# Third block of four: another order of the w1 quads, sums read in place, and a fifth group of w2 in seven products

## The chip, the core and the metric

One core of a Trainium2 chip runs the whole kernel. The metric is the device time of one execution in microseconds; the median of three runs is given. A kernel's profile comes from one further execution.

## What is computed

Cut to what matters (x has 2048 rows of 1024; 1024 states; w1 is 1024 x 3584, w2 is 3584 x 1024):

```python
xn = layernorm(x)
Lam_bar = exp(dt * Lam)                       # complex, one per state
Bu = xn @ (((Lam_bar - 1) / Lam)[:, None] * Bmat).T
h[t] = Lam_bar * h[t - 1] + Bu[t]             # recurrence over the 2048 rows
A = 2 * Re(h @ Cmat.T) + xn * Dskip
m = xn @ w1 + b1
B = (m * tanh(softplus(m))) @ w2              # mish, then the second layer
out = x + A + B
```

## The kernel before, in words

The 2048 rows are worked in four blocks of 512. In each block TensorE makes three kinds of product: the first layer (w1), the projections into and out of the recurrence (B and C), and the second layer (w2, called dense). Every product of 128 x 128 weights goes through PSUM, which has eight banks of 512 columns. VectorE does the recurrence: it rotates the projections (`rotate_in`, L914), scans them (`scan`, L1451), rotates back (`recur`, L1458). ScalarE applies mish, scales and evacuates banks.

The four blocks differ. The first multiplies plainly. In the second, four of seven quads of w1 are done with seven half-size products in place of eight; in the third and fourth all seven quads are, and the projections as well. A quad is a set of 512 rows of the hidden layer. Each of its seven products (n = 1 to 7) needs one unit of weights of 256 KB: n = 1, 2, 4 are raw pieces of w1, and n = 5, 7, 6, 3 are sums and differences of pieces, which VectorE makes once (`w_sums`, L1191). All units lie in DRAM (`wsd`), and each block fetches them again through a ring of seven slots of 512 KB, filled by SP (`ring_load`, L426; `ring_fill`, L856). A slot is refilled when PE has used it. An item of the ring is a pair of units, in the order of use.

The sums of quads 0, 1 and 2 are made in the third block itself: a step `k0` makes the next one on VectorE and POOL stores it (those of quad 2 are stored by SP, step `O0`). Before, the third block took the quads in the order 3, 4, 5, 6, 0, 1, 2 (`REAL`, L207), and fetched every unit from `wsd`, those just made too.

The second layer of the third and fourth block is done partly in seven products too. There the 28 tiles of the hidden layer are split in halves 0 to 13 and 14 to 27; a group is two tiles of each half. `NFG` (L186) says how many groups a block does in seven products: 4 in the third, all 7 in the fourth. The remaining tiles of the third block are multiplied plainly, in pairs (`PLAIN`, L189), 8 matmuls of 512 columns per tile. For the seven products a group's four rows of w2 are loaded raw by POOL (`d2_load`, L1219), scaled by ScalarE (`d2_row`, L1233), summed by VectorE (more `k0` steps) and stored in `w2d`; the hidden tiles are scaled (`act_scale`, L896) and summed (`act_sums`, L1339; `CHUNKS`, L1323). Group 4, which the fourth block needs, was made while its tiles passed through the ring in the third block's plain part (`PASSING`, L190).

The order of the third block is a string, `STEPS` (L196), of steps such as p1 (product 1 of the first quad; p q s w x y z are the seven quads in order of work, a b c d the projections), k0, g (mish), G (scale two hidden tiles), h (scale a row of w2), m (load rows of w2), r (rotate), E (statistics of the next block's x), l0 (load that x, by POOL), t (sums of the hidden tiles). A product and its evacuation were one step. What follows the last product stood in the code: `dense_part` (L1589) and the loop over `recur`. Its PE order is the seven products 1, 7, 2, 5, 6, then the plain pairs, then 3 and 4, then the projection out, j = 0 to 7.

Each engine runs its own instructions in the order in which the steps issue them, and waits on semaphores only where a buffer is not yet written or still read. Banks count as buffers: product 6 of a quad waits until product 1 in the same bank has been read out.

Of the kernel before, what the change touches and what calls it, by code (L numbers as in the profile page):

```python
# [9 lines left out]
P = 128  # L10
# [153 lines left out]
def build_kernel(nc, A_x, A_Lambda_re, A_Lambda_im, A_B_re, A_B_im, A_C_re, A_C_im,  # L164
# [27 lines left out]
    WHOLE = ("a2 a1 V0 b2 b1 a5 b5 V1 P4 P5 a6 b6 v6 P6 P7 a3 b3 P0 a7 b7 P1 Q0 n0 p1 q1 a4 b4 "  # L192
# [6 lines left out]
    LAST = ("p1 p5 p2 q1 q5 p6 q2 s1 p7 s5 p3 q6 s2 M5 p4 q7 q3 k0 k0 s6 q4 g0 K0 a2 a1 k0 s7 k0 s3 O0 O0 O0 O0 m6 b2 b1 s4 G1 G0 g1 a5 G3 b5 G2 a6 b6 "  # L199
# [7 lines left out]
    REAL = (3, 4, 5, 6, 0, 1, 2)  # L207
    UNITS = [(REAL[QUADS.index(o[0])], int(o[1])) for o in STEPS.split() if o[0] in QUADS]
    W_ITEMS = [("ws", tuple(UNITS[i:i + 2])) for i in range(0, len(UNITS), 2)]
    ON_CHIP = [(5, n) for n in (5, 6, 3, 7)]  # L210
    OPENS = [(REAL[QUADS.index(o[0])], int(o[1])) for o in WHOLE.split() if o[0] in QUADS]
    OPENS = [u for u in OPENS if u not in ON_CHIP]
    O_ITEMS = [("w1", f // 2) for f in TILES[::2]] + [("ws", tuple(OPENS[i:i + 2])) for i in range(0, len(OPENS), 2)]

# [197 lines left out]
    items = []  # L412
    for blk in range(NB):
        items += W_ITEMS if blk in SPLIT else O_ITEMS if blk == FAST else [("w1", g) for g in range(NF // 2)]
# [8 lines left out]
        items += [("c", j) for j in range(NJ)] if blk >= FAST else []  # L423
    n_loaded = [0]
# [175 lines left out]
    def plain_root():  # L600
        aop(lambda e: e.activation(ln[:, 3, :], mv[:, :, 1], AF.Sqrt, bias=kon[:, 2:3]), reads=b_mv + [b_kon], writes=b_ln[3])
        vop(lambda e: e.reciprocal(ln[:, 3, :], ln[:, 3, :]), reads=b_ln[3], writes=b_ln[3])
# [247 lines left out]
    n_item = [0]  # L850

    def item_done():
        n_item[0] += 1
        ring_fill()
# [8 lines left out]

    def first_tile(blk, f):
        bank = f % 8
        raw = blk == 0 and f < NR
        if raw:
            first_rest(f)
        for k in range(0 if raw else NK):
            s, w = w1_tile(n_item[0], f % 4, k)  # L870
            PE.mm(lambda e, k=k, w=w: e.matmul(ps[:, bank, :], lhsT=w, rhs=xnT[:, k, :],  # L871
                                               start=k == 0, stop=k == NK - 1),
                  reads=[b_ring[s]] + b_xnT, writes=[b_ps[bank]], first=k == 0, last=k == NK - 1)
        if f % 4 == 3:
            item_done()
            item_done()
        at = place(blk, f)
        ts = slice(2 * P if raw else 0, 4 * P)
        aop(lambda e: e.activation(at[0][:, ts], ps[:, bank, ts], AF.Mish, bias=b1(f)),
            reads=[b_ps[bank], b_par], writes=[at[1]])  # L880
# [113 lines left out]
    def w_out(blk, i, ci):  # L994
        f0 = 4 * i + 2 * ci
        return f0, *(places(SPLIT[0], f0, 2) if blk in SPLIT else places(blk, 4 * REAL[i] + 2 * ci, 2))

    def w_product(blk, i, n):
# [3 lines left out]
        direct = blk == FAST and (REAL[i], n) in ON_CHIP  # L1002
        if direct:
            unit, b_unit = w_unit(w_raw(REAL[i], *((1, 1), (0, 0), (0, 1), (1, 0))[(5, 6, 3, 7).index(n)]))
        else:
            kind, units = items[n_item[0]]
            s, half = n_item[0] % NRING, units.index((REAL[i], n))
            assert n_item[0] < n_loaded[0]
# [18 lines left out]
        if not direct and half == len(units) - 1:  # L1027
            item_done()

    def w_evacuate(blk, i, n, keep):  # L1030
        X, Y, Z = (F_BANKS if blk == FAST else W_BANKS)[i]
        at = REAL[i]
# [156 lines left out]
    steps, later, held = [], [], []  # L1189
# [21 lines left out]
    D2_RAW += [(("a", 24), ("a", 10)), (("h", 0), ("h", 4)), (("h", 8), ("h", 12))]  # L1211
# [21 lines left out]
    def d2_row(n, slot=None):  # L1233
# [4 lines left out]
        if slot is not None:  # L1238
            x, b_x = ring[:, slot, j * D:(j + 1) * D].rearrange("p (d t) -> p d t", d=2), [b_ring[slot]]
        aop(lambda e: e.activation(o, x, AF.Copy, scale=wg[:, r:r + 1]),  # L1240
            reads=b_x + [b_wg], writes=b_t[2 * j:2 * j + 2])
# [5 lines left out]

    def d2_scale(g):
        for n in range(4):
            d2_row(4 * g + n)  # L1250
# [72 lines left out]
    CHUNKS = {2: ((0, 8),), 3: ((0, 6), (6, 12), (12, 14))}  # L1323
# [44 lines left out]
    def project_fast(blk, order, open_unit):  # L1368
        keep = {}
        for o in order.split():  # L1370
            kind, n = o[0], int(o[1:])
            if kind == "r":
                rotate_in(n)
            elif kind == "u":
                open_unit(n)
            elif kind == "G":
                act_scale(blk, n)
            elif kind == "g":
                mish(blk, n)
            elif kind == "k":  # L1380
                if steps or later:
                    some(1)
                    ring_fill()
            elif kind == "e":
                if later:
# [654 lines left out]
```

## Time and profile before

| | |
|---|---|
| three timed runs, us | 588.10, 587.55, 587.74 |
| median, us | 587.74 |
| profiled execution: span, us | 586.3 (no other time of it is shown) |
| busy: VectorE, ScalarE, POOL | 88%, 69%, 26% of the span |
| granted TensorE clock | 1.000 |
| moved by DMA | 162.15 MB, mean 277 GB/s |

The span runs from the first to the last instruction of the profiled execution, the timed runs include what lies around it. Third block: from about 306.9 to 446.9 us. A line of a timeline gives the start in us, the time from the first start to the last end, the engine, the source line, the operation, the tiles written and read, and how many instructions were merged; a bracket says how long the engine had been idle and whom it waited for. Of a matmul, records can be missing.

### The profile page before, as it was taken

Reading aid. Unit: us, or ns where it says so; the run is one execution under the profiler, and the core shown is the slowest. Engines: PE = TensorE matmul, PEld = TensorE weight load, DVE = VectorE, ACT = ScalarE, POOL = GpSimd, SP = SyncE. Lnnn points to the kernel's source line nnn. Section 1 sums busy time; section 2 is a strip of 40 time slices with the busy share of each in tenths; the row PEclk is TensorE's granted clock in tenths of the full one; section 3 lists DMA queues with packets and bytes.
Section 4 is the critical chain, followed back from the end, with each engine's and each line's share of the span. In section 5 each row is a group of like instructions: output and inputs, shape, how many; then the busy total and the mean of one; then the engine's idle time right before and its main releaser. Section 6 shows DMA issues by size and latency. Waiting matters only on the chain.

```text
span 586.3 us, 9768 instructions
## 1 busy us (share of the span) xinstructions
PE 581.0 (99%) x3599; PEld 353.9 (60%) x3635; DVE 513.4 (88%) x789; ACT 401.8 (69%) x541; POOL 150.7 (26%) x213
## 2 busy tenths in 40 slices
PE   9999999999999999999999999999999999999998
PEld 8644444444447887444448888644446888844444
DVE  6998999998997878999877889779999669789995
ACT  4859994658578868999916687959223798992330
POOL 2899300123524420441351241001010113100000
PEclk9999999999999999999999999999999999999999
DMA  9999998999688978999999899798865966998832
GB/s 244 306 243 247 245 186 202 316 301 360 185 303 287 357 249 293 316 321 255 345 375 345 305 309 382 257 344 209 306 210 191 346 237 241 326 324 318 293 113 73
DMA packets 116345, 162.15 MB, mean 277 GB/s; under 512 B 55882, under 2 KB 66762, under 8 KB 116298
## 3 DMA queue, kind: packets, MB, share of 16 engines
q1 hardware_dynamic: 99776, 109.67, 62.0%
q0 software_dynamic: 13440, 44.57, 21.7%
q10 hardware_dynamic: 3082, 7.29, 3.3%
q8 instruction: 29, 0.48, 0.3%
q14 instruction: 18, 0.15, 0.1%
HBM read 115.36 MB, written 34.08 MB: 255 GB/s over the span
## 4 chain that ended last, share of the span: by engine, by line
PE 93%; DVE 2%; ACT 2%; DMA 1%; issue 1%; POOL 0%; ACTq 0%; POOLq 0%
PE ps L1502 34%; PE ps L1024 19%; PE ps L948 13%; PE ps L1563 10%; PE ps L871 10%; PE ps L1438 5%; DMA act<-in_A_B_im_dram 1%; PE ps L680 1%; PE ps L689 1%; PE ps L642 1%; ACT act L894 1%; PE ps L1525 1%; ACT act L901 1%; DVE CT L835 0%; DVE CT L833 0%
## 5 line engine op out<-in xcount | busy, mean ns | idle before, releaser
L1502 PE MATMUL ps<-ring,act 128*128 128x512 bf16 x532 | 117.3, 379 | 0.6
L1502 PEld LDWEIGHTS ps<-ring,act 128*128 128x128 bf16 x544 | 53.2, 98 | 63.8
L1044 ACT ACTIVATE snaps<-ps,par,cs 128x256 f32<-128x256 f32 x100 | 54.4, 562 | 44.4 <-PE ps L1024 40.0
L1502 PE MATMUL ps<-ring,hT 128*128 128x512 bf16 x355 | 78.3, 379 | 0.4
L1024 PE MATMUL ps<-TT,ring 128*128 128x256 f16 x552 | 68.3, 273 | 0.0
L910 DVE TENSOR_TENSOR mt<-hT,tab 128x2048 bf16<-128x2048 bf16 (+1 forms) x56 | 67.9, 1213 | 0.4
L1502 PEld LDWEIGHTS ps<-ring,hT 128*128 128x128 bf16 x362 | 35.4, 98 | 42.7
L1453 DVE TENSOR_TENSOR_SCAN hT<-cs,qi,hT 128x512 bf16<-128x512 f32 x48 | 60.7, 1275 | 0.0
L1024 PEld LDWEIGHTS ps<-TT,ring 128*128 128x128 f16 (+1 forms) x552 | 53.8, 98 | 7.2 <-issue 0.2
L871 PE MATMUL ps<-xnT,ring 128*128 128x512 bf16 x258 | 56.8, 379 | 0.3
L1024 PE MATMUL ps<-xnT,ring 128*128 128x256 bf16 x424 | 53.9, 273 | 0.0
L1061 DVE SCALAR_TENSOR_TENSOR act<-ps,cs,snaps 128x512 bf16<-128x512 f32 x54 | 39.8, 748 | 15.2 <-PE ps L1024 13.3
L1024 PEld LDWEIGHTS ps<-xnT,ring 128*128 128x128 bf16 (+1 forms) x424 | 41.4, 98 | 5.4
L871 PEld LDWEIGHTS ps<-xnT,ring 128*128 128x128 bf16 x264 | 25.8, 98 | 30.9
L1230 POOL DMA_DIRECT2D w2d<-act x21 | 15.0, 718 | 110.5 <-ACT act L1240 54.9
L1473 ACT ACTIVATE hT<-hT,wz 128x1024 bf16<-128x1024 bf16 x16 | 18.1, 1146 | 34.3 <-DVE hT L1468 34.3
L1563 PE MATMUL ps<-ring,act 128*128 128x512 bf16 (+1 forms) x176 | 39.5, 379 | 0.2
L1230 POOL DMA_DIRECT2D w2d<-hb x28 | 20.0, 717 | 74.4 <-ACT hb L1240 33.0
L894 ACT ACTIVATE act<-act 128x2048 bf16<-128x2048 bf16 (+3 forms) x13 | 33.0, 2557 | 3.8 <-DVE act L1047 3.8
L973 DVE TENSOR_TENSOR hT<-ps,snaps 128x512 f16<-128x512 f32 x36 | 23.8, 687 | 12.3 <-ACT snaps L965 11.1
L1563 PEld LDWEIGHTS ps<-ring,act 128*128 128x128 bf16 (+1 forms) x180 | 17.6, 98 | 20.6
L1173 POOL DMA_DIRECT2D wsd<-hb x35 | 19.1, 548 | 39.0 <-DVE hb L1199 28.8
(240 smaller groups left out, 1085.2 us busy)
## 6 DMA issues: line engine op xcount, KB each, us to landing
ring<-wsd SPq DMA_DIRECT2D x122, 256.0 KB, 4.6
ring<-in_B_w_dram SPq DMA_DIRECT2D x54, 512.0 KB, 5.9
ring<-ctd SPq DMA_DIRECT2D x24, 512.0 KB, 4.4
ring<-w2d SPq DMA_DIRECT2D x24, 512.0 KB, 4.6
wsd<-hb POOLq DMA_DIRECT2D x35, 256.0 KB, 5.1
ring<-w2d SPq DMA_DIRECT2D x29, 256.0 KB, 3.8
w2d<-hb POOLq DMA_DIRECT2D x28, 256.0 KB, 5.5
w2d<-act POOLq DMA_DIRECT2D x21, 256.0 KB, 6.2
```

The source lines that it names most:

```text
L871: PE.mm(lambda e, k=k, w=w: e.matmul(ps[:, bank, :], lhsT=w, rhs=xnT[:, k, :], start=k == 0, stop=k == NK - 1), reads=[b_ring[s]] + b_xnT, ...
L894: aop(lambda e: e.activation(t, t, AF.Mish), reads=b, writes=b)
L910: vop(lambda e: e.tensor_tensor(mt[:], u.unsqueeze(1).to_broadcast([P, 2, 2, TB]), tab[:, :, j, :].unsqueeze(2).to_broadcast([P, 2, 2, TB] ...
L948: PE.mm(lambda e, w=w, x=x, o=o, begin=begin, end=end: e.matmul(ps[:, bank, o:o + TH], lhsT=w, rhs=x, start=opens and begin, stop=end, ski ...
L1024: PE.mm(lambda e, w=w, x=x, o=o, begin=begin, end=end: e.matmul(ps[:, bank, o:o + TH], lhsT=w, rhs=x, start=opens and begin, stop=end, ski ...
L1044: aop(lambda e, o=o, p=p, j=j: e.activation(o, p, AF.Identity, scale=ig, bias=b1(f0 + j)), reads=[b_ps[b], b_par, b_ig], writes=b_dst)
L1061: vop(lambda e: e.scalar_tensor_tensor(out=dst, in0=bank(b), scalar=ig, in1=src, op0=ALU.mult, op1=ALU.add), reads=[b_ps[b], b_snap[k], b_ ...
L1230: PO.dma(lambda e: e.dma_start(w2d[at // 4][:, at % 4 * TB:(at % 4 + 2) * TB].rearrange("p (j t) -> p j t", j=2), t[:, :, d, :]), sem, rea ...
L1438: PE.mm(lambda e, j=j, ci=ci, k=k, bank=bank: e.matmul(ps[:, bank + ci, :], lhsT=BT[:, ci, j, k, :], rhs=xnT[:, k, :], start=k == 0, stop= ...
L1453: vop(lambda e: e.tensor_tensor_scan(out=hT[:, ci, j, :], data0=cj("r", j).to_broadcast([P, TB]), data1=hT[:, ci, j, :], initial=init, op0 ...
L1502: PE.mm(lambda e: e.matmul(ps[:, u, :], lhsT=lhsT, rhs=rhs, start=st_, stop=last, skip_group_check=blk in SPLIT), reads=reads, writes=[b_p ...
L1563: PE.mm(lambda e: e.matmul(ps[:, bank, :], lhsT=lhsT, rhs=rhs, start=st_, stop=end, skip_group_check=True), reads=b_t + [b_ring[s]], write ...
```

## The change

The third block's quads come in the order 3, 2, 0, 1, 4, 5, 6. The twelve products that use sums of quads 2, 0 and 1 read them where VectorE made them, and the ring no longer carries these units. The seven products of the second layer take a fifth group (tiles 8, 9, 22, 23), which leaves the plain part; group 4 of w2 is loaded raw and made earlier in the block (steps m4, h16 to h19). The whole kernel is now driven by such strings: a product p1 and its evacuation ep1 are separate steps, and the tail is written out (D and X are the seven products of the second layer, the first digit n; pl plain pairs, sc scans, to and so the rotation back, ta the last sum, al scales, sk and sx the next block's preparation, Y, Q and fin the projection out and the end). The strings of the first, second and fourth block are written from the code's former order. The ring's slots are freed by counting uses.

```diff
-    NFG = {2: 4, 3: GF}
-    W2_ORDER = (*range(9), 13, *range(9, 13))
-    EARLY, LATE = ((0, 18), (26, 28)), ((18, 26),)
-    PLAIN = [(f, f + 1) for f in (24, 10, 8, 22, 12, 26)]
-    PASSING = {8: 4, 22: 4}
-    SCALED_AT = {24: (8, 22), 10: (12,), 8: (26,)}
+    NFG = {2: 5, 3: GF}
+    W2_ORDER = tuple(range(14))
+    EARLY, LATE = ((0, 20),), ((20, 28),)
+    PLAIN = [(f, f + 1) for f in (24, 10, 12, 26)]
+    PASSING = {}
...
-    STEPS = ("p1 p5 p2 k0 k0 q1 k0 q5 p6 k0 q2 s1 k0 p7 s5 p3 k0 q6 s2 p4 k0 q7 q3 k0 s6 q4 m1 k0 g0 a2 a1 k0 s7 O0 s3 O0 b2 b1 k0 O0 s4 g1 k0 O0 a5 "
-             "b5 O0 a6 b6 O0 a3 h4 b3 S0 O0 a7 O0 h5 b7 k0 c2 d2 k0 h6 a4 b4 h7 l0 k0 c5 c1 k0 d5 d1 r0 c6 G0 c3 G1 d6 d3 c7 G2 w1 d7 r1 w5 w2 G3 c4 d4 k0 E0 E1 w6 x1 x5 x2 k0 w7 k0 w3 r2 "
-             "x6 w4 k0 y1 y5 y2 x7 x3 E2 E3 y6 x4 z1 z5 g2 z2 y7 y3 z6 G7 y4 g6 z3 z7 u0 t0 G8 u2 G9 z4 I2 G10 u1 t1 t2")
+    STEPS = ("p1 p5 ep1 ep5 p2 ep2 k0 k0 q1 eq1 p3 k0 q5 p6 q2 k0 ep6 eq2 s1 eq5 O0 k0 ep3 p7 es1 O0 ep7 s5 es5 k0 O0 q6 eq6 s2 es2 O0 p4 ep4 k0 q7 eq7 s6 "
+             "q3 eq3 k0 es6 q4 eq4 g0 k0 s7 s3 es7 o0 w1 ew1 es3 eb2 o0 s4 es4 k0 w2 m1 o0 b2 o0 k0 b1 w5 k0 ew2 a1 eb1 ew5 ea2 w6 ew6 w3 b5 eb5 ec2 g1 "
+             "ew3 w7 h4 ew7 a2 ea1 b6 eb6 w4 ew4 a5 b3 ea5 a6 eb3 h5 b7 ea6 S0 a3 k0 eb7 a7 ea7 m4 ea3 k0 d2 h6 ed2 G1 c2 a4 b4 h7 ea4 eb4 r0 c1 ec1 k0 c5 "
+             "ec5 d5 ed5 d1 c6 k0 ed1 ec6 c3 ec3 d6 G0 ed6 G2 d3 c7 r1 ed3 ec7 l0 x1 h16 d7 ed7 x5 E1 ex1 h17 c4 h18 E0 x2 h19 ex2 ec4 k0 y5 d4 ex5 ed4 E2 "
+             "x6 ex6 y1 y2 ey1 ey5 k0 ey2 x7 x3 ex7 ex3 y6 r2 x4 ey6 k0 ex4 k0 z1 z5 ez1 G3 ez5 k0 z2 k0 y7 y3 ez2 k0 z6 z3 ez6 ey7 ez3 g2 D11 G7 ey3 y4 "
+             "k0 ey4 z7 ez7 G8 g6 G9 D10 z4 t0 D70 E3 ez4 G10 t1 kp2 t2 r3 r4 D71 D20 lr0 g7 G12 kp0 D21 r5 G4 G5 X5 li0 X6 r6 kp1 G11 kp3 pl24 ns2 pl10 "
+             "ns0 r7 ns1 G6 G13 tr0 ns3 tr1 tr2 tr3 pl12 pl26 sc20 sc00 sc21 sc50 sc01 sc10 to0 sc11 so0 al0 ta0 X3 to1 so1 sc30 al1 to2 sc41 sc31 so2 to3 "
+             "sc60 sc40 al2 so3 sc71 to4 X4 so4 sc51 to5 so5 al4 sc70 al3 sc61 al5 to6 so6 jk0 to7 so7 sk0 al7 sk1 sk2 sk3 al6 Y0 sx0 sx1 sx2 sx3 Y1 Y2 Y3 "
+             "Y4 Y5 Q0 fin0 Q1 fin1 ax2 ax3 Q2 fin2 Q3 fin3")
...
-    REAL = (3, 4, 5, 6, 0, 1, 2)
+    REAL = (3, 2, 0, 1, 4, 5, 6)
+
+    def group(blk, i):
+        return REAL[i] if blk in SPLIT else i + 3
+
+    def fetched(blk, order, made):
+        us = [(group(blk, QUADS.index(o[0])), int(o[1])) for o in order.split() if o[0] in QUADS and len(o) == 2 and o[1].isdigit()]
+        us = [u for u in us if u not in made]
+        return [("ws", tuple(us[i:i + 2])) for i in range(0, len(us), 2)]
+
+    ON_CHIP = {FAST: [(5, n) for n in (5, 6, 3, 7)], SPLIT[0]: [(g, n) for g in (2, 0, 1) for n in (5, 6, 3, 7)], NB - 1: []}
...
-    D2_RAW += [(("a", 24), ("a", 10)), (("h", 0), ("h", 4)), (("h", 8), ("h", 12))]
+    D2_RAW += [(("h", 8), ("h", 12)), (("h", 0), ("h", 4)), (("h", 8), ("h", 12))]
...
-        direct = blk == FAST and (REAL[i], n) in ON_CHIP
+        g = group(blk, i)
+        direct = (g, n) in ON_CHIP[blk]
         if direct:
...
-    CHUNKS = {2: ((0, 8),), 3: ((0, 6), (6, 12), (12, 14))}
+    CHUNKS = {2: ((0, 10),), 3: ((0, 6), (6, 12), (12, 14))}
...
+    def used(i):
+        left[i] -= 1
+        if left[i] == 0:
+            gone.add(i)
+            return True
+        return False
+
+    def release():
+        while n_item[0] in gone:
+            n_item[0] += 1
+            ring_fill()
...
+        def pop_step():
+            if steps or later:
+                some(1)
                 ring_fill()
```

`act_scale` is not changed. The steps G4 and G11, which scale tiles 8, 9, 22 and 23, stand late in the string: G4 behind t2, G11 behind kp1.

More of the change, by code (lines that the diff above doesn't have):

```diff
@@ L862, in ring_fill @@
             ring_load()
[L864 to L880, printed above, removed]
     def places(blk, f, n):
@@ L1026, in w_product @@
                     reads=b_unit + b_x, writes=[b_ps[bank]], first=begin, last=end, chained=not opens)
-        if not direct and half == len(units) - 1:
-            item_done()
+        if not direct and used(at):
+            release()
     def w_evacuate(blk, i, n, keep):
         X, Y, Z = (F_BANKS if blk == FAST else W_BANKS)[i]
-        at = REAL[i]
+        at = group(blk, i)
         ig = wsm(3, at, at + 1)
@@ L1187, in w_scale @@
             w_keep(i, cis)
-    steps, later, held = [], [], []
+    steps, later, held, held_out = [], [], [], []
     def w_sums(i, later=False):
@@ L1239, in d2_row @@
             x, b_x = ring[:, slot, j * D:(j + 1) * D].rearrange("p (d t) -> p d t", d=2), [b_ring[slot]]
-        aop(lambda e: e.activation(o, x, AF.Copy, scale=wg[:, r:r + 1]),
-            reads=b_x + [b_wg], writes=b_t[2 * j:2 * j + 2])
+        put = ((lambda e: e.activation(o, x, AF.Copy, scale=wg[:, r:r + 1])) if queue is AC else
+               (lambda e: e.tensor_scalar(o, x, wg[:, r:r + 1], None, op0=ALU.mult)))
+        queue.op(put, reads=b_x + [b_wg], writes=b_t[2 * j:2 * j + 2])
         if n % 4 == 3:
@@ new lines, in perform @@
+        for o in (FIRST, WHOLE, STEPS, LAST)[blk].split():
+            kind = o.rstrip("0123456789.")
+            arg = o[len(kind):]
+            if kind in ("D", "X"):
+                a = arg.split(".")
+                ks = range(int(a[1]), int(a[2])) if len(a) > 1 else range(ng)
+                n, i = (int(a[0][0]), (int(a[0][1]),)) if kind == "D" else (int(a[0]), (0, 1))
+                rows(n, i, ks)
+            elif len(kind) == 1 and kind in QUADS:
+                w_product(blk, QUADS.index(kind), int(arg))
+            elif len(kind) == 1 and kind in "abcd":
+                product(blk, "abcd".index(kind), int(arg))
+            elif len(kind) == 2 and kind[0] == "e" and kind[1] in QUADS:
+                w_evacuate(blk, QUADS.index(kind[1:]), int(arg), keep)
+            elif len(kind) == 2 and kind[0] == "e" and kind[1] in "abcd":
+                evacuate("abcd".index(kind[1:]), int(arg), keep, kind[1:] in "ab" and blk != FAST)
+            else:
+                run[kind](int(arg or 0))
@@ L2005, in build_kernel @@
+        assert near or not (steps or later), (len(steps), len(later))
+    for blk in range(NB):
+        perform(blk)
     SP.wait(out_events.values())
```

783 lines of the change are left out of this document (278 added, 505 removed), and 30 rows, old and new, of tables (FIRST, LAST, WHOLE).

## Prediction

> **What bounds the kernel now.** I read the page's first part, then the waits of PE, then the chain in order of time, then each engine's timeline over the third block.
>
> ```profile
> span 586.3 us, 9768 instructions
> PE 581.0 (99%) x3599; PEld 353.9 (60%) x3635; DVE 513.4 (88%) x789; ACT 401.8 (69%) x541; POOL 150.7 (26%) x213
> ```
> ```profile
> PE ps L642 <- DVE filler L468: 1.0, 1, 1.0
> PE ps L680 <- ACT xr L527: 0.2, 1, 0.2
> ```
>
> PE is busy for 581.0 of 586.3 us, and the two lines are all the waiting of matmuls that the profile names, both in the first microseconds. So the kernel is as long as its list of matmuls, and a part of the change counts only if it shortens that list or makes PE wait.
>
> ```profile
> 306.85 15.84 PE ps L1024 x144
> ...
> 352.53 20.96 PE ps L1024 x192
> ...
> 394.27 10.74 PE ps L1502 x49
> 405.06 7.29 PE ps L1502 x33
> ...
> 446.88 15.72 PE ps L1024 x144
> ```
> ```profile
> L1502 PE MATMUL ps<-ring,act 128*128 128x512 bf16 x532 | 117.3, 379 | 0.6
> L1502 PEld LDWEIGHTS ps<-ring,act 128*128 128x128 bf16 x544 | 53.2, 98 | 63.8
> ```
>
> The first and last of the chain's lines bound the third block: 446.88 - 306.85 = 140.03 us. Records of matmuls are missing (532 against 544 weight loads), so 49 of them stand for 50: one of 512 columns costs (405.06 - 394.27) / 50 = 0.216 us. One unit's product (8 matmuls of 256 columns, 192 records being 24 products) costs 20.96 / 24 = 0.873 us. Check: the block has 77 such products and 112 + 96 + 128 = 336 wide matmuls; 77 x 0.873 + 336 x 0.216 = 139.8 of 140.03. There is next to no idle time to win.
>
> **What goes and what comes on PE.** The pairs (8, 9) and (22, 23) leave the plain part: 4 tiles x 8 units = 32 matmuls. In the seven products each gains two steps of k on two banks: 7 x 2 x 2 = 28. Net: 4 fewer, 4 x 0.216 = 0.86 us. The new order of the quads changes no count, nor do direct units: the matmul is the same, only its weights lie elsewhere. The other three blocks keep their PE order.
>
> **What moves beside it.** Twelve 256 KB loads from wsd (sums of quads 2, 0, 1), and two 512 KB loads of w2 leave SP's queue; seven 256 KB loads of w2d come. The stores of those sums stay, as the fourth block reads them. POOL gets two raw loads of 512 KB (m4). I cost this at nothing, since PE never waited with the larger list. The price of being wrong is in the rivals.
>
> ```profile
> 337.33 1.41 DVE L1261 TENSOR_TENSOR act<-act 128x1024 f16<-128x1024 bf16 x2
> 352.87 1.41 DVE L564 BATCH_NORM_STATS2 stats<-xx 128x6 f32<-128x512 bf16 x2
> 371.95 1.11 DVE L1047 TENSOR_SCALAR act<-ps,cs,par 128x256 bf16<-128x256 f32 x2
> 372.98 1.40 DVE L1061 SCALAR_TENSOR_TENSOR act<-ps,cs,snaps 128x512 bf16<-128x512 f32 x2
> 379.50 2.49 DVE L1363 TENSOR_TENSOR act<-act 128x2048 f16<-128x2048 bf16 x2 [0.52 <-ACT act L901]
> 383.83 1.40 DVE L1580 SCALAR_TENSOR_TENSOR KS<-ps,wz,xx 128x512 f32<-128x512 f32 x2
> 389.33 1.22 DVE L910 TENSOR_TENSOR mt<-hT,tab 128x2048 bf16<-128x2048 f16 x1
> 391.37 1.22 DVE L910 TENSOR_TENSOR mt<-hT,tab 128x2048 bf16<-128x2048 f16 x1
> 397.70 3.63 DVE L1453 TENSOR_TENSOR_SCAN hT<-cs,qi,hT 128x512 bf16<-128x512 f32 x3
> ```
>
> *The block's start.* Product q5 now needs a sum of quad 2. It is PE's sixth product, at 306.85 + 5 x 0.873 = 311.2. VectorE joins p2 after PE ends it at 309.5 (0.70), and then makes the sum (0.7): 310.9. Cover 0.3 us; the later sums of the three quads stand two products ahead or more.
>
> *Products x to z.* Four tensor_scalar-like operations of group 4 (h16 to h19) come to ScalarE and four sums to VectorE, which stood in the tail before. The sums for the seven products grow from 8 to 10 tiles: 1.25 to about 1.55 us each (estimate from the 379.50 row, by size). From the first statistics (E1, behind x5) to the evacuation of z4, VectorE has: four statistics of 1.6 us (two reads and a small end), nine joins of 0.70, eight sums of 0.70, one rotation of 2.04 (391.37 - 389.33), three evacuations of 1.11 and one sum of 1.55: 25.2 us, about 1 less where issues overlap. x5 ends on PE at 306.85 + 56 x 0.873 = 355.7, and the join before E1, of the product before that, is done at about 355.6. The bank of D71 must be read out by ez4 first, and D71 starts at 306.85 + 77 x 0.873 + 30 x 0.216 = 380.5. So VectorE arrives between 379.8 and 380.8: from 0.7 us early to 0.3 late. I take the early end, as pairs in these rows take less than twice one. This is the tightest place.
>
> *The tail.* From there VectorE has until the sum before X3 (ta0): two sums of 1.55, five rotations of 2.04, two pairs of KS of 1.40, seven scans of 1.21, the turn 1.2, its two sums 0.7, one more sum 1.55, small ones 0.3: 28.3 us, hence 408.1 to 409.1. X3 starts at 380.5 + 70 x 0.216 + 64 x 0.216 = 409.4. Cover 0.3 us or more.
>
> ```profile
> 427.33 2.19 DVE L1261 TENSOR_TENSOR act<-act 128x1024 f16<-128x1024 bf16 x3
> ```
>
> Behind X3 VectorE is lighter than before, because these 2.19 us, group 4's sums, have gone from its list.
>
> *ScalarE before X5.* The square root (lr0) now stands ahead of the last mish (g7), and G4 stands behind both; the order leaves G4 and G11 behind the sums that now read tiles 8, 9, 22 and 23, so those enter the seven products before their scale, and X5 now waits for G4.
>
> ```profile
> 369.02 3.60 ACT L894 ACTIVATE act<-act 128x4096 bf16<-128x4096 bf16 x1
> 379.37 1.24 ACT L1586 ACTIVATE KS<-ps,wz 128x512 f32<-128x512 f32 x2
> 380.51 1.90 ACT L894 ACTIVATE act<-act 128x2048 bf16<-128x2048 bf16 x1
> 382.44 2.56 ACT L901 ACTIVATE act<-act,wz 128x512 bf16<-128x512 bf16 x4
> 392.74 1.28 ACT L601 ACT_TABLE_LOAD   x1
> 394.03 0.30 ACT L601 ACTIVATE ln<-mv,kon 128x4 f32<-128x4 f32 x1
> ```
>
> From 369.02 to 379.4 ScalarE did g2, g6 and four scales; that chain starts about 1 us later now, so at 380.4. Then: KS 1.2, two tables 2.6, root 0.3, mish 1.9, G12 and G4 2.6: 389.0. X5 starts at 380.5 + 30 x 0.216 = 387.0 and comes to tile 8 after 16 matmuls, at 390.5. Cover 1.5 us.
>
> The Trainium skill, "ScalarE: Activation LUTs", section "What ACT_TABLE_LOAD costs", states that a switch takes about 1.28 us of load and some 1.38 us of drain besides. The rows show the load (1.28) and the root 0.01 us behind it, so I take 1.28.
>
> **The sum.** The profiled execution's span is 586.3 us; less 0.86 it is 585.4. No time of that execution other than its span is shown; the three timed runs have a median of 587.74 us, 1.4 above the span. That distance stays: 587.74 - 0.86 = 586.9 us. Less than 0.2% (1.18 us) can't be told from no change in this kernel, so the likeliest case counts as the same.
>
> **Rivals.**
>
> *VectorE waits for the next block's x (slower).* E1 reads x that POOL fetches at l0. Before, there lay 352.87 - 341.96 = 10.9 us between load and reading, and the loads needed nearly all of it:
>
> ```profile
> 341.96 2.20 POOL L398 DMA_DIRECT2D xx<-in_A_x_dram  x4
> ```
> ```profile
> L398 POOL DMA_DIRECT2D xx<-in_A_x_dram x4: 539/548/584, 342.0 to 343.6; - x4
> ...
> DMA to landing us min/median/max: 10.0/10.7/11.3
> ```
> ```profile
> L398 POOL DMA_DIRECT2D xx<-in_A_x_dram x4: 539/548/584, 236.5 to 238.1; - x4
> ...
> DMA to landing us min/median/max: 4.3/4.9/6.7
> ```
>
> Now l0 stands behind the store of a sum that VectorE makes after c6, at about 350; the second load issues at about 351.3, and E1's turn comes at 355.6. At 4.9 us (the second row, from the second block) E1 waits 0.6 us, which is what cover there is; from about 5 us on every microsecond goes through the 24 to 25 us of VectorE's list to D71 and to PE. At 7.4 us (between the rows) PE loses 2.4: 589.3 us. At 10.7 it loses 5.7: 592.6. For it: half the distance of before. Against: the slow loads lay among stores on SP and POOL and ring loads, and now, with the ring full of x to z and products a to d needing none, the queue should be nearly empty at 350. Chance 0.2.
>
> *Small waits eat the gain (no change).* Any of the tight places (q5, D71, X3) misses by some tenths, or the second operand of D70 comes late: group 4's sum for it is made at about 369, is stored, then fetched. Two stores of w2d from hb between 357 and 360 us landed in the first line's times, five loads of w2d to the ring between 376 and 380 us in the second's:
>
> ```profile
> DMA to landing us min/median/max: 5.2/5.4/5.6
> ```
> ```profile
> DMA to landing us min/median/max: 2.6/3.4/4.6
> ```
>
> 369.7 + 5.4 + 3.4 = 378.5; D70 comes to that tile at 378.4 + 8 x 0.216 = 380.1: cover 1.6 us. Together I put 0.9 us on such waits: 587.74 - 0.86 + 0.9 = 587.8. Chance 0.2.
>
> *The tables cost more.* If each switch held ScalarE as long again as its load (1.28 us), G4 would end at 391.6 and X5 would wait 1.1 us: 588.0, still the same by the bound. The row at 394.03 speaks against. Chance 0.03. That case is the Trainium skill's rule named above; the trace here doesn't agree with its drain.
>
> *More than the four matmuls goes (faster).* The check above leaves 0.2 us of idle time in the block, and timed runs spread by 0.5; 0.4 us more would make 586.5. Chance 0.1.
>
> The forecast itself has 0.47. Low end 586.4 (the last case); high end 588.9, which takes in the small waits, the tables and the first rival up to 7 us. Faster by over 0.2%: 0.1, slower: 0.2 (the first rival), the rest the same.
>
> **What would show it.** Right: the third block, from the first product p1 to the fourth block's, takes 139.1 to 139.3 us; PE still names no wait there; E1 starts below 356.5; D71 follows D70 at once. First rival: DVE waits for a DMA to xx before its statistics, and a gap of PE before y2 or D71. Small waits: PE idle for tenths at q5, D70, D71 or X3. Tables: ScalarE idle or a drain beside its table loads, and X5 interrupted. The forecast is wrong if the block shortens by well over 0.9 us, if the block lengthens, or if time moves in another block, whose order I take to be unchanged.

## The result, and the profile after

| | before | after |
|---|---|---|
| timed runs, us | 587.55 to 588.10 (6 runs) | 588.67 to 594.39 (6 runs) |
| median, us | 587.79 | 591.90 |
| profiled execution: span, us | 586.3 | 590.6 (that execution's time: 591.81) |

After to before: 1.0063, with a 95% interval of 1.0043 to 1.0083. By the medians the change makes the kernel slower by about 4.1 us, outside the predicted range of 586.4 to 588.9 us, and its runs spread over 5.7 us where those of before spread over 0.6. G4 and G11 stand behind sums and products that read their tiles, so these read tiles 8, 9, 22 and 23 unscaled; that holds for the changed kernel and for all variants of it below but those that say otherwise. Three single runs far off the rest (609.01 and 1252.82 us of the kernel before, 877.06 us of one variant) are left out of the ratios.

First the page of the changed kernel, then all waits of its matmuls. (Lines have moved: L1544 are the matmuls of the second layer, L1063 the products of w1's units, L1676 the end of a block, L1238 the sums for w1, L1297 the sums for w2's groups.)

```profile
span 590.6 us, 9767 instructions
PE 582.7 (99%) x3631; PEld 353.0 (60%) x3631; DVE 511.2 (87%) x784; ACT 402.0 (68%) x541; POOL 151.9 (26%) x215
```
```profile
PE ps L1544 <- DMA ring<-w2d: 1.9, 2, 1.1
PE ps L1063 <- DVE xx L1676: 1.4, 1, 1.4
PE ps L1063 <- DVE act L1238: 1.3, 1, 1.3
PE ps L675 <- DVE filler L499: 1.0, 1, 1.0
```

The last line was there before; the other three are new, 4.6 us in all. "99%" hides them: the share is that of a whole run. The timeline of PE has their places:

```profile
308.29 1.03 PE L1063 MATMUL ps<-xnT,ring 128*128 128x256 bf16 x8 [1.43 <-DVE xx L1676]
...
314.08 1.05 PE L1063 MATMUL ps<-TT,act 128*128 128x256 f16 x8 [1.27 <-DVE act L1238]
...
381.38 0.60 PE L1544 MATMUL ps<-ring,S 128*128 128x512 f16 x2
383.04 1.04 PE L1544 MATMUL ps<-ring,S 128*128 128x512 f16 x4 [1.06 <-DMA ring<-w2d]
384.94 1.25 PE L1544 MATMUL ps<-ring,S 128*128 128x512 f16 x5 [0.87 <-DMA ring<-w2d]
...
451.00 1.04 PE L1063 MATMUL ps<-xnT,ring 128*128 128x256 bf16 x8
```

In order: p1, the first product of the third block, which waits 1.43 us; q5, which reads a sum where VectorE made it, 1.27; D70 twice, 1.93. The same timeline of the kernel before has the fourth block's start at 446.72:

```profile
446.72 1.04 PE L1024 MATMUL ps<-xnT,ring 128*128 128x256 bf16 x8
```

It begins at 451.00 now, 4.28 us later. The new waits less the four matmuls give 4.63 - 0.86 = 3.8. The remaining 0.5 us lies beside the waits: in these rows a group of matmuls starts up to 0.17 us before the one ahead of it ends, and behind a wait that overlap is lost (p1 began at 306.68 before, 1.61 us earlier, for 1.43 us of idle time).

Two of the three waits have their cause ahead of the third block. VectorE must make four sums for a group of w2 before it ends the second block's rows (L1676). The first fence is of before, the second of after:

```profile
296.88 2.93 DVE L1261 TENSOR_TENSOR act<-act 128x1024 f16<-128x1024 bf16 x4
```
```profile
304.06 2.94 DVE L1297 TENSOR_TENSOR act<-act 128x1024 f16<-128x1024 bf16 x4 [7.10 <-DMA w2d<-act]
306.92 4.61 DVE L1676 TENSOR_TENSOR xx<-ps,xx 128x1024 bf16<-128x1024 f32 x4
```

They come 7.2 us later, and what VectorE does behind them comes late too. Followed back (a sum waits for the store of the raw rows, the store for ScalarE, ScalarE for POOL's load), this ends at the start of one load, POOL's first for group 2. Again before, then after:

```profile
276.06 0.72 POOL L1225 DMA_DIRECT2D act<-in_B_w_dram  x1 [5.38 <-PE ps L1502]
```
```profile
272.62 0.72 POOL L1264 DMA_DIRECT2D act<-in_B_w_dram  x1 [1.93 <-PE ps L1544]
```

The load starts *earlier*. It waits for tiles 20 to 23, which the second block's plain products read; the natural W2_ORDER has them done one pair sooner. At 272.55 SP had just issued a DMA transpose of the third block's x, and at 274.95 it issued the next. DMA from 268 to 290 us (transfers, size, median us from issue to landing), before and after:

```profile
ring<-ctd SPq DMA_DIRECT2D x5, 512.0 KB, 6.6
act<-in_B_w_dram POOLq DMA_DIRECT2D x4, 512.0 KB, 8.3
xnT<-xn SPq DMA_TRANSPOSE x2, 5.1
```
```profile
ring<-ctd SPq DMA_DIRECT2D x5, 512.0 KB, 13.0
act<-in_B_w_dram POOLq DMA_DIRECT2D x4, 512.0 KB, 12.9
xnT<-xn SPq DMA_TRANSPOSE x2, 12.1
```

All three kinds take longer: the two transposes 12.1 in place of 5.1 us, the rows 12.9 in place of 8.3. In this stretch all DMA together moved 201 GB/s in place of 307, at about the same busy share of its engines (1.01 and 0.99). The early load itself still landed a little sooner, at 283.1 in place of 283.8 us. But a group's two loads share a semaphore, so ScalarE waits for the second, issued at 279.65 in both kernels; it took 12.0 us in place of 7.1 (ScalarE before, then after):

```profile
286.82 8.41 ACT L1240 ACTIVATE act<-act,cs 128x1024 bf16<-128x1024 bf16 x8
```
```profile
291.63 4.27 ACT L1279 ACTIVATE act<-act,cs 128x1024 bf16<-128x1024 bf16 x4 [4.72 <-DMA act<-in_B_w_dram]
```

So an early start went with late data. Whether one is the cause of the other, two traces can't say.

### The profile page after: what moved, and what is told of

It reads as the page before. It is cut to its first block, busy times and chain, and to the rows that moved or that the text cites. A ratio compares the mean times of both kernels' runs of the same rounds, so it can differ in the third digit from the quotient of the medians.

```text
span 590.6 us, 9767 instructions
## 1 busy us (share of the span) xinstructions
PE 582.7 (99%) x3631; PEld 353.0 (60%) x3631; DVE 511.2 (87%) x784; ACT 402.0 (68%) x541; POOL 151.9 (26%) x215
## 4 chain that ended last, share of the span: by engine, by line
PE 88%; DMA 5%; DVE 3%; ACT 3%; issue 1%; POOL 0%; DVEq 0%
PE ps L1544 44%; PE ps L1063 15%; PE ps L985 11%; PE ps L1755 10%; PE ps L1773 5%; DMA act<-in_B_w_dram 2%; DMA w2d<-act 1%; PE ps L713 1%; DMA ring<-w2d 1%; PE ps L722 1%; DMA w2d<-hb 1%; DVE xx L1676 1%; ACT act L1279 1%; ACT hb L1279 1%; PE ps L675 1%
## 5 line engine op out<-in xcount | busy, mean ns | idle before, releaser
L1544 PE MATMUL ps<-ring,act 128*128 128x512 bf16 (+1 forms) x716 | 156.2, 379 | 0.0
L1544 PEld LDWEIGHTS ps<-ring,act 128*128 128x128 bf16 (+1 forms) x716 | 70.0, 98 | 83.3 <-DMA ring<-w2d 0.2
L1544 PE MATMUL ps<-ring,hT 128*128 128x512 bf16 (+1 forms) x390 | 83.4, 376 | 0.0
L1544 PEld LDWEIGHTS ps<-ring,hT 128*128 128x128 bf16 x390 | 38.1, 98 | 45.0
L1063 PE MATMUL ps<-TT,ring 128*128 128x256 f16 x480 | 59.8, 273 | 0.0
L1063 PE MATMUL ps<-xnT,ring 128*128 128x256 bf16 x400 | 50.4, 273 | 1.4 <-DVE xx L1676 1.4
L1063 PEld LDWEIGHTS ps<-TT,ring 128*128 128x128 f16 (+1 forms) x480 | 46.8, 98 | 6.5
L1269 POOL DMA_DIRECT2D w2d<-hb x35 | 25.0, 716 | 87.4 <-ACT hb L1279 50.4
L1063 PEld LDWEIGHTS ps<-xnT,ring 128*128 128x128 bf16 (+1 forms) x400 | 38.9, 98 | 6.8 <-issue 1.9
L938 ACT ACTIVATE act<-act,cs 128x512 bf16<-128x512 bf16 x48 | 30.8, 708 | 0.1
L1766 ACT ACTIVATE act<-ps,par 128x512 bf16<-128x512 f32 (+1 forms) x40 | 23.6, 660 | 8.2 <-PE ps L1755 8.2
L1223 ACT ACTIVATE hb<-hb,cs 128x2048 bf16<-128x2048 bf16 x10 | 19.4, 1995 | 14.1 <-DVE xx L1676 12.7
```

Of the source, the lines that this page charges most:

```text
L938: aop(lambda e, a=a, y=y: e.activation(a, a, AF.Copy, scale=y), reads=[b_a, b_y], writes=[b_a])
L1063: PE.mm(lambda e, w=w, x=x, o=o, begin=begin, end=end: e.matmul(ps[:, bank, o:o + TH], lhsT=w, rhs=x, start=opens and begin, stop=end, ski ...
L1269: PO.dma(lambda e: e.dma_start(w2d[at // 4][:, at % 4 * TB:(at % 4 + 2) * TB].rearrange("p (j t) -> p j t", j=2), t[:, :, d, :]), sem, rea ...
L1544: PE.mm(lambda e: e.matmul(ps[:, bank, lo:hi], lhsT=lhsT, rhs=rhs, start=opens, stop=last, skip_group_check=split), reads=reads, writes=[b ...
```

## The experiments

Each kernel was run in turn with the kernel before on the same chip; the ratio is to that. Theory A: the early load among the transposes makes p1 and q5 late. Its rival: the transposes are slow by chance, or by something else in the change. Theory B: D70's operand is late because of what its load waits for. Its rival: the added transfers slow the loads.

**The old order of w2's pairs (A).**

```diff
-    W2_ORDER = tuple(range(14))
-    EARLY, LATE = ((0, 20),), ((20, 28),)
+    W2_ORDER = (*range(9), 13, *range(9, 13))
+    EARLY, LATE = ((0, 18), (26, 28)), ((18, 26),)
```

> The changed kernel, with the pairs of w2 in the second block back in the order before (0 to 8, 13, 9 to 12), nothing else touched. Theory A (the natural order frees tiles 20 to 23 one pair earlier, POOL's load of w2 rows for group 2 then starts at 272.6 in place of 276.1 us, falls on the DMA transposes of the third block's x, and what ScalarE and VectorE make from those rows comes late, so that p1 and q5 wait 2.7 us in all): the load is back at about 276, the transposes take about 5 us in place of 12, VectorE's four sums start at about 297 in place of 304, and p1 and q5 wait for nothing; only D70's wait of 1.9 us is left: 588.5 to 589.2. Rival B (the slow transposes come at random, or from something else in the change): the transposes stay at about 12 us in some runs, time 591 to 592 and its spread of several us as before.

Measured 588.76 us against 587.92, ratio 1.0015 (1.0006 to 1.0024). The load, the transposes and the sums are back, and the waits of p1 and q5 are gone (its lines of POOL, DMA and PE's waits):

```profile
276.10 0.72 POOL L1264 DMA_DIRECT2D act<-in_B_w_dram  x1 [5.38 <-PE ps L1544]
```
```profile
xnT<-xn SPq DMA_TRANSPOSE x2, 6.1
```
```profile
PE ps L675 <- DVE filler L499: 1.0, 1, 1.0
PE ps L1544 <- DMA ring<-w2d: 0.9, 2, 0.7
```

Of the two waits for w2d that are left, 0.20 us lie at D70 and 0.66 at the ninth matmul of D20. This execution took 587.71 us, the lowest of the eleven, so the others lost about 1 us more (by the median), and no trace shows where. By the medians, this order alone carries 3.3 of the 4.1 us (4.1 less 588.76 - 587.92).

**The natural order, the load later (A).** Only the halves of group 2's rows change places, so that the first load waits for the last pair.

```diff
+    D2_RAW[2] = (("a", 24), ("a", 20))
```

> The changed kernel with its natural order of w2's pairs kept, and only the two halves of group 2's raw rows exchanged between tiles 20 to 23 and 24 to 27, so that POOL's first load waits for the last pair of the second block and starts at about 279.6 in place of 272.6 us. Theory A (it is the start of this load among the transposes that costs): transposes of about 5 us, no wait at p1 and q5, D70's wait alone left: 588.4 to 589.5. Rival (the natural order itself costs, by its sizes or its ring): p1 and q5 wait as in the changed kernel, 590.5 to 592.

Measured 588.64 against 587.60, ratio 1.0018 (1.0008 to 1.0028), as with the old order. So the order by itself costs nothing that can be told; the load's start does.

```profile
279.94 2.85 POOL L1265 DMA_DIRECT2D act<-in_B_w_dram  x4 [8.83 <-PE ps L1545]
```
```profile
xnT<-xn SPq DMA_TRANSPOSE x2, 4.7
```

**The kernel before, with the load earlier (A).**

```diff
-    D2_RAW = [... ("a", 20), ("a", 8)]
+    D2_RAW = [... ("a", 18), ("a", 8)]
```

> The kernel before, with group 2's rows of w2 loaded into tiles 18 to 25 in place of 20 to 27, so that the first raw load may start one pair of w2 earlier, as in the changed kernel; nothing else touched. Theory A (an early load falls on the transposes): the load starts at about 272.5 in place of 276, the transposes take some 12 us in place of 5, VectorE's four sums come at about 304 in place of 297, and p1 waits 1 to 2 us (q5 needs no such sum in this order): 589 to 590. Rival B: the transposes stay at about 5 us and the time at 587.8.

Measured 590.08 against 587.92, ratio 1.0043 (1.0019 to 1.0067), runs from 587.82 to 594.69. Nothing else of the change is in this kernel, and its profile shows the slow transposes, the late sums and a late p1. Five of the twelve runs lie within those of the kernel before (587.23 to 589.16), so the early load doesn't cost in every run. Its POOL, DMA and waits:

```profile
273.03 0.72 POOL L1225 DMA_DIRECT2D act<-in_B_w_dram  x1 [1.93 <-PE ps L1502]
```
```profile
xnT<-xn SPq DMA_TRANSPOSE x2, 12.7
```
```profile
PE ps L1024 <- DVE xx L1711: 2.3, 1, 2.3
```

Theory A stands: put in alone it slows the kernel, taken out in two different ways it is gone. The rival falls.

**One semaphore split, alone and with the old order (B).** Group 4's sums for products 5, 7 and 6 shared a semaphore of three stores, so the load of sum 7 waited for the store of sum 6 too.

```diff
-        sem = DmaSem(nc, "d_ts%d" % g, nper=3)
-        last = DmaSem(nc, "d_tu%d" % g)
+        sem = DmaSem(nc, "d_ts%d" % g, nper=2 if g == 4 else 3)
+        last = DmaSem(nc, "d_tu%d" % g, nper=2 if g == 4 else 1)
...
-                d2_store(g, n, h, d, last if n == 4 else sem)
+                d2_store(g, n, h, d, last if n == 4 or (g, n) == (4, 6) else sem)
```

> The changed kernel, with the stores of group 4's sums for products 5 and 7 on one semaphore and those for 6 and 4 on another, so that the ring's load for D70 no longer waits for the store of the sum after it. Theory (D70 is late because its load waits for that store): the load starts 2 to 4 us earlier, PE's wait of 1.9 us at D70 goes: about 590. Rival (the slot of the ring, or the load itself, sets the time): D70 waits as before and the time stays at 591 to 592.

> The changed kernel with both of the other edits: the old order of w2's pairs in the second block, and the split semaphore. If both theories hold, PE has no wait in the third block and the time is what was predicted first, 586.7 to 587.2, below the kernel before (587.8). If only the order matters, 588.5 to 589.2; if only the semaphore, about 590.

Alone: 591.16 against 587.92, ratio 1.0049 (1.0028 to 1.0070). With the old order: 588.89 (588.55 without the run of 877.06), ratio 1.0007 (0.9998 to 1.0016), where the old order alone had 1.0015 (1.0006 to 1.0024). Neither is told apart from the kernel without the split: inconclusive. In the profiled execution of both, D70 still waited 2.2 us: its second load began earlier (374.88 in place of 375.76) but took 7.1 us. And the waits were not the whole loss. Behind them the granted clock stood at 0.50, from about 382 to 385 us, and 14 matmuls took 4.78 us, where the run with the old order alone took 3.20 for the same 14 (this run, then that one):

```profile
382.02 4.78 PE L1544 MATMUL ps<-ring,S 128*128 128x512 f16 x14 [1.04 <-DMA ring<-w2d]
```
```profile
380.02 3.20 PE L1544 MATMUL ps<-ring,S 128*128 128x512 f16 x14 [0.20 <-DMA ring<-w2d]
```

All variants from here on have the old order of w2's pairs too.

**Group 4's sums earlier on VectorE (B).**

```diff
-... x5 E1 ex1 h17 c4 h18 E0 x2 h19 ex2 ec4 k0 y5 d4 ex5 ed4 E2 x6 ...
+... x5 k0 k0 ex1 h17 c4 h18 k0 k0 x2 h19 ex2 ec4 k0 y5 d4 ex5 ed4 k0 k0 x6 ...
```

The three statistics E1, E0 and E2 take the places of these sums.

> The changed kernel with the old order of w2's pairs in the second block, and on VectorE the sums of groups 1 and 4 moved ahead of the statistics E1, E0, E2 of the next block's x (those take the places of the sums). Group 4's sum for D70 is then made at about 362 in place of 369.4 us and its load to the ring can start some 4 to 7 us earlier. Theory (with the first load of group 2 back, all that is left is D70's late operand): no wait of PE at D70, nor anywhere in the third block: 586.8 to 587.2, 0.7 to 1.1 below the kernel before. Rival (D70's load is slow because other transfers run beside it, whenever it starts; or VectorE becomes late for the evacuation of z4): PE still waits 0.9 to 2 us at D70 or D71, 588.2 to 589.

A miss: 596.84 against 587.60, ratio 1.0154 (1.0140 to 1.0168). VectorE:

```profile
368.06 2.94 DVE L1297 TENSOR_TENSOR hb<-hb 128x1024 f16<-128x1024 bf16 x4 [8.57 <-DMA w2d<-hb]
```

The sum overwrites rows that are still being stored, and VectorE stood 8.57 us for that store; PE waited 7.5 us for VectorE, and the granted clock stood at 0.50 from 368 to 376 us. So the chain (rows, store, sum, store, load) can't be shortened at the sum alone. Two variants of the same kernel, with the scales ahead and with the split besides, failed alike:

> The kernel with the early group 4, and in it the scales of tiles 8, 9, 22 and 23 moved ahead of the sums that read them (G4 into an idle stretch of ScalarE near 344 us, G11 behind G10, and the rotation r3 ahead of t1 to cover it); in the changed kernel these four tiles enter the seven products of the third block unscaled. If ScalarE and VectorE have the room that their idle time suggests, it is as fast as the kernel with the early group 4, within 0.3 us; if G11 (1.3 us) stands on the path to t1, X5 and the sum before X3, it is 1 to 1.3 us slower than that.

> The kernel with the early group 4 and the scales ahead, and group 4's stores on two semaphores as well, so that D70's load doesn't wait for the sum after it. If the early sums already cover D70, the split changes nothing: the same time as the kernel with the scales ahead, within 0.3 us. If D70 is still late there, this one is up to 1 us faster.

They took 597.54 and 597.31, ratios 1.0164 (1.0150 to 1.0178) and 1.0163 (1.0149 to 1.0177).

**Rows h16 to h19 earlier on ScalarE (B).**

```diff
-... d6 G0 ed6 G2 d3 c7 r1 ed3 ec7 l0 x1 h16 d7 ed7 x5 E1 ex1 h17 c4 h18 E0 x2 h19 ...
+... d6 h16 ed6 h17 h18 d3 c7 r1 ed3 ec7 l0 x1 h19 d7 ed7 x5 k0 k0 k0 k0 ex1 G0 c4 E1 x2 G2 ...
```

VectorE's order behind x5 is changed with it: group 1's sums, then E1 and E0, then group 4's, with E2 last.

> The changed kernel with the old order of w2's pairs in the second block; ScalarE scales group 4's rows (h16 to h19) about 3 to 4 us earlier, in the places of the scales G0 and G2, which come after them; VectorE makes group 1's sums first, then two statistics, then group 4's sums, ahead of the rotation r2. Unlike the first try at this, the sums stand some 6 us behind the stores of the raw rows that they overwrite. Theory (group 4 is late because its chain rows, store, sum, store, load starts late): its sums come at about 364 in place of 368 us, D70's load about 4 us earlier, and PE has no wait from p1 to the fourth block: 586.8 to 587.3, 0.4 to 1 below the kernel before. Rival (the sums wait again for the stores of the raw rows): VectorE waits for a DMA at about 363 us and PE with it, 588 or more.

> The same, with the scales of tiles 8, 9, 22 and 23 ahead of the sums that read them (G4 at about 344 us, G11 behind G10, the rotation r3 ahead of t1); in the changed kernel and the others of this study these four tiles enter the seven products of the third block unscaled. If the idle time of ScalarE and the cover behind t1 suffice, within 0.3 us of the one without; if G11 stands on the path, 1 to 1.3 us more.

> The kernel with the early rows, and group 4's sums 5, 7 on one semaphore, 6 and 4 on another. If the early rows cover D70, the same time as without, within 0.3 us. If D70 or the products behind it still wait for a load there, up to 1 us faster, or no faster if the load's own 4 to 7 us set it.

588.58, 588.52 and 588.96 against 587.81; ratios 1.0017 (1.0006 to 1.0027), 1.0010 (1.0002 to 1.0019), 1.0020 (1.0010 to 1.0030). In the profiled executions VectorE no longer waits for a store, and D70 waits for no load; instead the last two matmuls of D11 wait 0.9 to 2.1 us for w2d. Putting the scales in costs nothing that can be told here.

**D7's last groups behind D2 (B).** The ring's items go in the same order.

```diff
-... D70 E3 ez4 G10 t1 kp2 t2 r3 r4 D71 D20 lr0 g7 G12 kp0 D21 r5 ...
+... D70.0.6 E3 ez4 G10 t1 kp2 t2 r3 D20 r4 D71.0.6 lr0 g7 G12 D21 D70.6.10 D71.6.10 kp0 r5 ...
```

> The changed kernel with the old order of w2's pairs in the second block, and product 7 (D7) of the second layer cut in two: its first three groups where they were, product 2 (D2, whose operands are raw rows and need no sum) next, and the last two groups of D7 behind D2; the ring carries the items in that order. Group 4's sum is made, stored and loaded as in the changed kernel, but needed some 4 to 6 us later. Theory (after the load of group 2, the rest of the loss is D70 waiting for a store and a load that can't be hurried): no wait of PE from p1 to the fourth block, 586.8 to 587.3, 0.5 to 1 below the kernel before. Rival (the transfers that the fifth group adds slow the ring's other loads, so that PE waits at another item): PE waits 0.5 to 2 us for w2d at another product, 588 to 589.

> The same, with the scales of tiles 8, 9, 22 and 23 ahead of the sums and products that read them (G4 at about 344 us, G11 behind G10, the rotation r3 ahead of t1), which the changed kernel leaves out of the seven products. If ScalarE and VectorE have the room, the same time as without within 0.3 us; if not, up to 1.3 us more.

589.58 against 587.88, ratio 1.0032 (1.0021 to 1.0044), and with the scales 591.19, 1.0052 (1.0036 to 1.0067). Slower, but this run gave the clue: PE waited at D70's *third* matmul, and SP's queue for 3.6 us. That item holds a sum of group 1, not of group 4. Group 1's sum 7 is stored early, but shares its semaphore with sum 6, which the new order of VectorE has put behind r2. With the scales D20, which stands earlier here, waits 1.32 us for ScalarE in place of 0.52.

**Two semaphores split (B).** As above, for groups 1 and 4 (`g in (1, 4)`).

> The changed kernel with the old order of w2's pairs, and the split semaphore for the sums of groups 1 and 4 (5 and 7 apart from 6 and 4), nothing moved. In the run with the old order alone the ring's load for D70's second pair of steps began at 371.94 us, when the store of group 1's sum 6 (made behind r2) had landed, though D70 needs sum 7, stored some 5 us before. Theory (that store, not group 4 alone, holds SP's queue): SP's first wait goes from 371.9 to about 368.3, the loads behind it start earlier, D70's first wait goes, and at most the one for group 4 is left: 587.2 to 588. Rival (the loads' own 4 to 7 us): 588.5 to 589 as with the old order alone.

588.08 against 587.85, ratio 1.0002 (0.9994 to 1.0011). One of SP's two waits for stores is gone, the other is left (SP's waits from 350 to 395 us, then a line of PE's waits, again at the ninth matmul of D20; D11 waited 0.6 us for VectorE besides):

```profile
SPq L481 <- DMA w2d<-hb: 4.8, 1, 4.8
```
```profile
PE ps L1544 <- DMA ring<-w2d: 0.9, 1, 0.9
```

**Then the sum for D70 ahead of two others (B).** On top of the two splits.

```diff
-            later.append(step)
+            later.insert(2 + (5, 7).index(n) if g == 4 and n in (5, 7) else len(later), step)
```

> The changed kernel with the old order of w2's pairs, the split semaphores of groups 1 and 4, and VectorE's order of four sums behind r2 turned: group 4's sums 5 and 7 first, then group 1's 6 and 4, so that the sum for D70 is made at about 368 in place of 369.4 us and its store is the second of four in POOL's queue, not the last. Theory (in the run with split semaphores SP still waited 4.8 us for that one store, and PE 0.9 us for an item behind it): SP's wait falls to about 2 us and PE's wait goes: 587.0 to 587.6, just below the kernel before. Rival (transfers beside one another, 5.6 us to landing for those stores, set it): 588.0 to 588.4 as with the split alone.

> The same, with the scales of tiles 8, 9, 22 and 23 ahead of the sums and products that read them (G4 at about 344 us, G11 behind G10, the rotation r3 ahead of t1). With the early rows this cost nothing (588.5 against 588.6); so within 0.3 us of the one without, or 1 to 1.3 us more if G11 is on the path here.

587.88 against 587.95, ratio 0.9999 (0.9990 to 1.0007); with the scales 588.20, 1.0002 (0.9991 to 1.0014). The same two lines, without the scales:

```profile
SPq L481 <- DMA w2d<-hb: 2.3, 1, 2.3
```
```profile
PE ps L1544 <- DMA ring<-w2d: 0.5, 1, 0.5
```

Step by step SP's wait falls (4.6 in two, 4.8, 2.3 us) and the time with it (588.76, 588.08, 587.88), though single steps are near what the measurement can tell. This is as far as these runs come: no version beats the kernel before.

**The whole chain of group 4 earlier (B against its rival).** m4 goes ahead of a sum at which POOL blocks, h16 to h19 into 344 to 354 us, the stores ahead of l0; the sums of groups 1 and 4 come earlier, and group 4 has the split semaphore.

```diff
-... S0 a3 k0 eb7 a7 ea7 m4 ea3 k0 ... h7 ea4 ... d6 G0 ed6 G2 d3 c7 r1 ed3 ec7 l0 x1 h16 ...
+... S0 m4 a3 k0 eb7 a7 ea7 ea3 k0 ... h7 h16 h17 ea4 ... d6 h18 ed6 l0 h19 d3 c7 r1 ed3 ec7 x1 ...
```

> The changed kernel with the old order of w2's pairs in the second block, and the whole chain of group 4 earlier: POOL's raw load m4 issued before it blocks on a sum of group 3, ScalarE's rows h16 to h19 between 344 and 354 us in place of 353 to 358.5, their stores ahead of the load of the next block's x, group 1's four sums at 356 to 359 and group 4's from 361 to 365, with group 4's sums 5 and 7 on a semaphore of their own. SP is idle until about 355 us, so most of these stores are through before the ring's loads for the seven products start. Theory (D70's loads wait for the stores of the sums of groups 1 and 4, which come late): no wait of PE for w2d from p1 to the fourth block: 586.8 to 587.3. Rival (the added transfers slow the loads wherever they lie): 0.9 to 2 us of waits for w2d, 588 to 589.

> The same, with the scales of tiles 8, 9, 22 and 23 ahead of the sums and products that read them (G4 at about 345 us, G11 behind G10, the rotation r3 ahead of t1). If the cover behind t1 suffices, within 0.3 us of the one without; if not, up to 1.3 us more.

589.44 against 587.85, ratio 1.0026 (1.0015 to 1.0038); with the scales 590.17, 1.0034 (1.0021 to 1.0047). SP waits for no store any more, but the rival's sign is there. The stretch from 360 to 372 us (busy time of PE, PEld, VectorE, ScalarE and POOL, clock, DMA share, GB/s), of before and of this kernel, and then PE's waits just behind it:

```profile
360.00:372.00 12.00, 12.00 (x112) 10.76 (x110) 10.35 (x19) 9.97 (x15) 0.72 (x1) 1.00 0.99 361
```
```profile
360.00:372.00 12.00, 11.89 (x110) 10.53 (x109) 11.29 (x21) 10.38 (x18) 2.85 (x4) 1.00 1.03 390
```
```profile
373.44 1.04 PE L1544 MATMUL ps<-ring,act 128*128 128x512 bf16 x4 [0.72 <-DMA ring<-w2d]
374.78 0.60 PE L1544 MATMUL ps<-ring,act 128*128 128x512 bf16 x2 [0.30 <-DMA ring<-w2d]
```

DMA moves 390 GB/s, loads of the ring take 5.5 to 6.0 us to land (4.2 with the old order alone), and D11 waits. So B and its rival each hold in part: hurried, the loads land later among the fifth group's transfers; not hurried, a load waits for their stores.

## Why the prediction was wrong, by its steps

*The step that failed: "The other three blocks keep their PE order."* They did not. W2_ORDER, which the change edits, is the order of the second block's second layer, and with it one load moved from 276.06 to 272.62 us. I had listed the DMAs that the third block gains and loses, and no queue of another block. Three variants (the old order, the later load, the early load alone) put the larger part here, 3.3 of the 4.1 us by the medians. The prediction did name this as its way to be wrong ("if time moves in another block, whose order I take to be unchanged"), but gave it no chance.

*The cover of D70, 1.6 us: mis-sized.* In the run with the old order the sum came when I said (about 369), a store took 4.6 us and the load 4.2 (I took 5.4 and 3.4); in the changed kernel the load took 6.3. Missed were four things. The load waited for the next sum's store as well (370.99 + 4.6 = 375.6, where I had 375.1 for the store alone). Its ring item also carries group 3's unit, which PE reads two steps of k sooner. Group 1's sum 6, ahead of r2 in the kernel before, came behind it and held SP's queue. And "What moves beside it" counted loads, but not the seven stores of group 4, which stood at 406 to 463 us before: from 355 to 395 us POOL stores eleven pieces of w2d from hb, where it stored three. "Small waits" had 0.9 us for all that, hence 587.8; the old order alone shows 588.76, and only the last two versions come near it (588.08 and 587.88).

*Right: the shorter list.* With waits taken out, the block lasts about what was worked out. In the last version it goes from 307.12 to 447.09 us, 139.97, of which PE waits 0.5: 139.4, against 139.1 to 139.3.

*Right: VectorE from E1 to z4.* 358.80 to 383.41 is 24.6 us (worked out: 24.2 to 25.2), so the wait at D71 that this would bring did not come. The first rival, x late at E1, with its chance of 0.2, was not seen in the changed kernel:

```profile
xx<-in_A_x_dram POOLq DMA_DIRECT2D x4, 256.0 KB, 4.2
```

4.2 us in place of 10.7: the loads landed fast, as was argued against it. At 5.1 us in the last version and 4.9 with the split and the old order, VectorE did wait at E1, 0.95 and 0.78 us (0.6 was worked out for 4.9). In the last version PE had no wait at D71 for all that, but VectorE was done at 381.08 and D71 began at about 381.2.

*Right: the tables and the tail.*

```profile
384.71 1.28 ACT L632 ACT_TABLE_LOAD   x1
386.00 0.30 ACT L632 ACTIVATE ln<-mv,kon 128x4 f32<-128x4 f32 x1
```

The root follows its table by 0.01 us, and X5 and X3 wait for nothing. The drain that the Trainium skill ("ScalarE: Activation LUTs", section "What ACT_TABLE_LOAD costs") adds to a switch is not seen here either.

*What stays open.* In the last version 0.86 us of matmuls are gone and 0.5 us of waiting has come in the profiled execution. Its block starts 0.44 us later than before (307.12 against 306.68), as the first block waited 0.39 us for a load there. By medians nothing is left of the gain, and whether this is so in the other runs is not shown. Why the transfers slow one another among the transposes was not tried either. The Trainium skill ("DMA: Bandwidth & Descriptors", section "Queues, rings and completion order") states that a DMA engine serves its queues in turn, packet by packet; that fits the direction, but no run here shows the turns. Turns alone also don't say why the total fell from 307 to 201 GB/s.

## What to carry to other kernels

Before calling a block unchanged, look who else reads a table or an order that is edited, and compare every engine's and queue's instructions of all blocks. A load that may start earlier is not a gain by itself: ask what is in flight at that moment, and who needs that more. Where several transfers share a semaphore or loads share a queue, the item that is waited for is the last of them, so work added anywhere ahead can make an untouched operand late. And before the waits of one profile are taken for the loss, see where that execution stands among the runs.

## What was not expected of the hardware

A 512 KB load that POOL issued between two DMA transposes (0.07 us behind the first), in place of 1.1 us behind the second, went with transposes of 12.1 in place of 5.1 us (12.7 when put into the kernel before), and with loads of SP's queue in the same stretch of 13.0 in place of 6.6 us. The load itself landed only 0.7 us sooner for its start 3.4 us earlier. The three kernels with it spread over 5.7 to 7.4 us between runs, those without over about 4.5 and less.

The granted clock of TensorE fell behind some waits of PE, to 0.50, as shown for two variants above. Other waits, of 1.4 us in the changed kernel's profile and 2.3 us in the kernel before with the early load, show no such fall, so what decides is not shown. In a run's mean clock it shows as 0.991 to 0.997; 0.003 of 590 us is an estimated 1.8 us. Two of the six runs of the changed kernel (594.39 and 591.99 us) have 0.997, as five of the twelve of the kernel before with the early load have 0.994 or 0.997 (all five above 592 us); no run of the kernel before with a clock on record has less than 1.000. So part of what the early load costs, and of the spread, is not waiting but a lower clock; how much of the 4.1 us is not shown.
